# A spectral mixing layer and its MLP: 47 x 64 against 94 x 32 as the factors of the transform

## The chip, the core and the metric

One core of a Trainium2 chip runs the program. The metric is the device time of one execution in microseconds; for the kernel before it is the median of three runs.

## The reference

```python
def _attn_ref(x, filt_r, filt_i):            # x (8, 3008, 256)
    X = np.fft.rfft(x, axis=1)
    F = (filt_r + 1j * filt_i)[None, :, :]   # (1505, 256)
    return np.fft.irfft(X * F, n=x.shape[1], axis=1)

def _moe_ref(x, w_in, w_out, alpha):         # x (24064, 256), w_in (256, 2048), w_out (2048, 256)
    h = x @ w_in
    g = np.maximum(h, 0.0) + alpha * np.minimum(h, 0.0)
    return g @ w_out
```

Each of eight batches is filtered along its 3008 positions in the frequency domain, channel by channel. The 24064 rows that result go through a two-layer MLP whose activation has one negative slope per hidden unit.

## The kernel before

**The transform.** 3008 = 47 x 64. Stage A (piece_a, L158) multiplies by a 47-point table for two halves of the 64 positions at once (94 rows, 96 columns out). The result is saved to DRAM (save_a, L167) and read back turned (turn_a, L171), so that positions lie on partitions. Stage B (piece_b, L180) is a 64-point transform with the twiddles in its table, a 128-by-128 complex table per frequency k1, two k1 per piece, twelve pieces a batch. DVE multiplies the result in PSUM by the filter twice (L188, L189), once for the plain and once for the crossed parts; POOL's DMA swaps the two 64-partition halves of the crossed product (L191); piece_s (L194) adds it. Stage C (piece_c, L199) is the inverse 64-point transform; turn_c (L212) turns it through DRAM. Stage D (piece_d, L226) is the inverse 47-point transform and leaves the batch transposed in yT. ACT takes A, C and D out of PSUM.

**Batch 0** (class First, L246) is done alone at the start, without DRAM: its turns are matmuls with an identity (turn_at, piece_t), its B computes plain and crossed parts with tables of 64 columns (L281), its C multiplies by two tables (L298, L299). warm() issues matmuls with no use but to keep PE running.

**The MLP.** Tokens go in 48 blocks of 512 (384 in one of twelve). A block has 16 steps. At step j, Block.up (L409) makes hidden tile j: two matmuls of 512 columns (L414) into one half of a PSUM tile hps. After every odd j ACT copies both halves to SBUF as fp16 (L420, 128 x 1024), and DVE applies the slope (L423 twice, L424). Block.down (L427) of the block before runs in the same steps: each step does 4 of the 64 matmuls of 256 columns (L433) that make the output, 16 to a group of 128 tokens, two groups in one PSUM tile `op`. When a tile is full (j = 7 and j = 15 in a block of 512) ACT copies it to osb (L438) and SP's DMAs store it.

**Order.** The code is in manual schedule: engines run in the order in which the program records. A plan (put, plan_fft, L444 to L486) lists pieces by step; in the loop at L490 the pieces of a step are recorded first, then up, then down. One batch's transform is spread over about 150 steps, ahead of its MLP, which begins at step 96 b.

**PSUM.** It has eight banks, used as pools: psH (two tiles of two banks, hps), psO (two tiles of one bank, `op`), psF (two tiles of one bank, all pieces of the transform through bank(), L142). A new tile of a pool takes the next buffer in turn and waits for the readers of what was there.

Of the kernel before, what the change touches and what calls it, by code (L numbers as in the profile page):

```python
# [14 lines left out]
N1 = 47  # L15
N2 = 64
NK1 = 24
D = 256
NB = 8
DFF = 2048  # L20
NH = 32
# [4 lines left out]
def _build_consts():  # L26

    s1 = np.arange(N1)
    s2 = np.arange(N2)
    k1 = np.arange(NK1)
    p = np.arange(64)
    k2 = np.where(p < 32, p, 95 - p)
    g = np.where(p < 32, 1.0, -1.0)

    a1 = 2 * np.pi * np.outer(s1, k1) / N1
    wf1 = np.zeros((2 * N1, 96))  # L40
    wi3 = np.zeros((96, 2 * N1))
    scale = np.where(k1 == 0, 1.0, 2.0) / NFFT
    for h in range(2):
        r = slice(h * N1, h * N1 + N1)
        wf1[r, h * 48 : h * 48 + NK1] = np.cos(a1)
        wf1[r, h * 48 + NK1 : h * 48 + 48] = -np.sin(a1)
        wi3[h * NK1 : h * NK1 + NK1, r] = (np.cos(a1) * scale).T
        wi3[48 + h * NK1 : 48 + h * NK1 + NK1, r] = (-np.sin(a1) * scale).T

    kk = k1[:, None] + 47 * k2[None, :]  # L50
    ang = 2 * np.pi * s2[:, None, None] * kk[None, :, :] / NFFT
    c, s = np.cos(ang), np.sin(ang)
    twf = np.empty((128, NK1, 128))
    twf[:64, :, :64], twf[64:, :, :64] = c, s
    twf[:64, :, 64:], twf[64:, :, 64:] = -s * g, c * g
    ec, es = c.transpose(2, 1, 0), s.transpose(2, 1, 0)
    gp = g[:, None, None]
    twi = np.empty((128, NK1, 128))
    twi[:64, :, :64], twi[:64, :, 64:] = ec, es
    twi[64:, :, :64], twi[64:, :, 64:] = -es * gp, ec * gp  # L60
    return wf1, wi3, twf, twi
# [3 lines left out]
def kernel(  # L65
# [11 lines left out]
    wf1_np, wi3_np, twf_np, twi_np = _build_consts()  # L77
    wf1_d = nc.inline_tensor(wf1_np.astype(np.float16), name="c_wf1")
    wi3_d = nc.inline_tensor(wi3_np.astype(np.float16), name="c_wi3")
    twf_d = nc.inline_tensor(twf_np.astype(np.float16), name="c_twf")  # L80
    twi_d = nc.inline_tensor(twi_np.astype(np.float16), name="c_twi")
    twx_np = np.concatenate([twi_np[64:], -twi_np[:64]])
    twx_d = nc.inline_tensor(twx_np.astype(np.float16), name="c_twx")
    id_d = nc.inline_tensor(np.eye(128, dtype=np.float16), name="c_id")
    wfx_np = wf1_np.reshape(2 * N1, 2, 2, NK1).transpose(0, 3, 2, 1).reshape(2 * N1, 96)
    wfx_d = nc.inline_tensor(np.ascontiguousarray(wfx_np).astype(np.float16), name="c_wfx")
# [4 lines left out]
    p_uw = ctx.enter_context(tc.tile_pool(name="p_uw", bufs=3))  # L91
# [3 lines left out]
    psO = ctx.enter_context(tc.tile_pool(name="psO", bufs=2, space=bass.MemoryType.PSUM))  # L95
    psF = ctx.enter_context(tc.tile_pool(name="psF", bufs=2, space=bass.MemoryType.PSUM))
    dram = ctx.enter_context(tc.tile_pool(name="dram", bufs=1, space=bass.MemoryType.DRAM))
    a_dram = dram.tile([NB, 96, NH, D], FP16, name="a_dram")
    v_dram = dram.tile([NB, 96, NH, D], FP16, name="v_dram")
# [3 lines left out]
    wf1_s = konst.tile([2 * N1, 96], FP16, name="wf1_s")  # L103
    wi3_s = konst.tile([96, 2 * N1], FP16, name="wi3_s")
    twf_s = konst.tile([128, NK1, 128], FP16, name="twf_s")
    twi_s = konst.tile([128, NK1, 128], FP16, name="twi_s")
    filt_s = konst.tile([128, NK1, D], FP16, name="filt_s")
    filts_s = konst.tile([128, NK1, D], FP16, name="filts_s")
# [6 lines left out]
    wfx_s = konst.tile([2 * N1, 96], FP16, name="wfx_s")  # L115
    id16 = konst.tile([128, 128], FP16, name="id16")
    gtb = konst.tile([128, 17, 2, 512], FP16, name="gtb")
    twx_s = gtb[:, 14:17].rearrange("p a b c -> p (a b c)").rearrange("p (k m) -> p k m", m=128)
    yT = konst.tile([128, 2, 2 * NFFT], FP16, name="yT")

    def xrow(b, h, c):
        return bass.AP(tensor=x.tensor, offset=x.offset + (b * NFFT + NH * h + 8 * c) * D,
                       ap=[[N2 * D, N1], [1, 8 * D]])

    def load_x(b, c):
        xs = p_x.tile([2 * N1, 8 * D], FP16, name="xs")
        for h in range(2):
            nc.gpsimd.dma_start(out=xs[h * N1 : h * N1 + N1], in_=xrow(b, h, c))  # L128
        return xs

    def load_filt(dst, pbase, src, ka, kb):
        n = kb - ka
        nc.gpsimd.dma_start(
            out=dst[pbase : pbase + 32, ka:kb],
            in_=bass.AP(tensor=src.tensor, offset=src.offset + ka * D,
                        ap=[[47 * D, 32], [D, n], [1, D]]))
        nc.gpsimd.dma_start(
            out=dst[pbase + 32 : pbase + 64, ka:kb],
            in_=bass.AP(tensor=src.tensor, offset=src.offset + (N1 - ka) * D,
                        ap=[[47 * D, 32], [-D, n], [1, D]]))  # L140

    def bank(wide=False):  # L142
        if wide:
            return psH.tile([128, 2, 512], FP32, name="hps")[:, 0]
        return psF.tile([128, 512], FP32, name="psF")


    class Fft:
        def __init__(self, b):
            self.b = b  # L150
            self.base = (b % 2) * NFFT
            self.px, self.uw = {}, {}

        def start_a(self):
            self.asb = p_fft.tile([96, NH, D], FP16, name="asb")
            self.at = p_fft.tile([128, NK1, D], FP16, name="at")

        def piece_a(self, i, evict, wide=False):  # L158
            if i == 0:
                self.start_a()  # L160
            xs = xc[(self.b, i // 4)]
            ps = bank(wide)
            o = (i % 4) * 512
            nc.tensor.matmul(ps[0:96], wf1_s, xs[:, o : o + 512], start=True, stop=True)  # L164
            evict(self.asb[:, 2 * i : 2 * i + 2].rearrange("p a d -> p (a d)"), ps[0:96])
# [5 lines left out]
        def turn_a(self, eng, ka=0, kb=NK1):  # L171
            for h in range(2):
                for c in range(2):
                    r = h * 48 + c * NK1
                    q = c * 64 + NH * h
                    eng.dma_start(
                        out=self.at[q : q + NH, ka:kb],
                        in_=a_dram[self.b, r + ka : r + kb].rearrange("k s d -> s k d"))

        def piece_b(self, kp):  # L180
            px = bank().rearrange("p (k d) -> p k d", k=2)
            for kh in range(2):
                k1 = 2 * kp + kh
                nc.tensor.matmul(px[:, kh], twf_s[:, k1], self.at[:, k1], start=True, stop=True)  # L184
            uu = p_uw.tile([128, 2, D], FP16, name="uu", bufs=4)
            ww = p_uw.tile([128, 2, D], FP16, name="ww")
            sw = p_uw.tile([128, 2, D], FP16, name="sw")
            nc.vector.tensor_mul(ww, px, filts_s[:, 2 * kp : 2 * kp + 2])  # L188
            nc.vector.tensor_mul(uu, px, filt_s[:, 2 * kp : 2 * kp + 2])  # L189
            for o in (0, 64):  # L190
                nc.gpsimd.dma_start(out=sw[o : o + 64], in_=ww[64 - o : 128 - o])  # L191
            self.uw[kp] = uu, sw

        def piece_s(self, kp):  # L194
            uu, sw = self.uw[kp]
            nc.vector.tensor_add(uu, uu, sw)  # L196
            self.uw[kp] = (uu,)

        def piece_c(self, kp, evict, pv=None):  # L199
            if kp == 0:  # L200
                self.v = p_fft.tile([128, NK1, D], FP16, name="v")
                self.zt = p_fft.tile([96, NH, D], FP16, name="zt")
            us = self.uw.pop(kp)
            if pv is None:
                pv = bank().rearrange("p (k d) -> p k d", k=2)
            for kh in range(2):
                k1 = 2 * kp + kh
                for u in us:
                    nc.tensor.matmul(pv[:, kh], twi_s[:, k1], u[:, kh], start=u is us[0], stop=u is us[-1])  # L209
            evict(self.v[:, 2 * kp : 2 * kp + 2], pv)  # L210

        def turn_c(self, q):  # L212
            k = 6 * q
            for h in range(2):
                for c in range(2):
                    r = c * 48 + h * NK1 + k
                    p = c * 64 + NH * h
                    nc.sync.dma_start(
                        out=v_dram[self.b, r : r + 6].rearrange("k s d -> s k d"),
                        in_=self.v[p : p + NH, k : k + 6])  # L220
            if q == 3:
# [4 lines left out]
        def piece_d(self, i, evict, wide=False):  # L226
            g, dh, mh = i // 4, (i // 2) % 2, i % 2
            pd = bank(wide)
            ps = pd[:, 0 : 8 * N1].rearrange("p (m x) -> p m x", m=4)
# [3 lines left out]
            t0 = self.base + g * 752  # L233
# [117 lines left out]
    for i in range(16):  # L351
        f0.piece_a(i, both[i % 2], i % 2 == 1)
        if i % 4 == 3:
            warm((16, 6, 5, 8)[i // 4])
# [178 lines left out]
```

## Time and profile before

| | |
|---|---|
| median of three runs | 798.21 us (797.52 to 799.13) |
| the profiled execution, its span | 797.5 us |
| busy: PE, DVE, ACT, POOL | 98%, 81%, 75%, 18% |
| ACT: L420, 384 times | 385.4 us, 1004 ns each |
| DVE: L188 and L189, 84 times each | 57.4 and 57.1 us, 683 and 679 ns each |
| PE: L164 (A), L184 (B), L209 (C), L231 (D) | 42.6, 32.0, 33.4 and 41.9 us |
| start of the first L414 matmul | 39.37 us |
| granted PE clock, each slice | 9 (90% or more) |

Times of single instructions are those of the profile's groups; a PE matmul's row contains the drain after its last column, so matmuls that follow each other overlap in the rows. The profile numbers lines of the kernel. "PEld" is the load of a matmul's stationary operand. "Idle before" of a row is the time in which its engine stood still ahead of it, with what ended it.

### The profile page before, as it was taken

How to read it: one execution, taken by the hardware profiler on the slowest of the kernel's cores; microseconds unless marked ns; L12 is line 12 of the kernel's file. 1: busy time of each engine (PE TensorE's matmuls, PEld its weight loads, DVE VectorE, ACT ScalarE, POOL GpSimd, SP SyncE). 2: the span in 40 equal slices, each digit the busy share in tenths (PEclk: the TensorE clock that was granted, in tenths of full speed). 3: DMA queues.
4: the chain of work that ended last, by engine and by line, in shares of the span. 5: the costliest groups of instructions: out<-in, count | busy, mean ns of one | idle time of the engine just before them, and what ended most of it. 6: DMA issues, size and time to landing. Idle time of an engine off the chain costs nothing.

```text
span 797.5 us, 16176 instructions
## 1 busy us (share of the span) xinstructions
PE 778.6 (98%) x5980; PEld 542.8 (68%) x5980; DVE 645.7 (81%) x1449; ACT 597.6 (75%) x836; POOL 141.5 (18%) x272
## 2 busy tenths in 40 slices
PE   6999999999999999999999999999999999999997
PEld 6756667666667666766667666766666766776665
DVE  4787996798879987798877988799877999777773
ACT  3678678877778887788768877788877867686663
POOL 7511330132103210132102321032100221000000
PEclk9999999999999999999999999999999999999999
DMA  9967448574655447474483545754484243511111
GB/s 179 211 143 181 132 106 223 157 169 115 150 153 121 110 125 173 126 142 129 119 207 83 119 127 141 177 112 113 123 179 117 54 106 85 138 38 28 41 40 53
DMA packets 94360, 100.59 MB, mean 126 GB/s; under 512 B 11369, under 2 KB 82041, under 8 KB 94217
## 3 DMA queue, kind: packets, MB, share of 16 engines
q1 hardware_dynamic: 79512, 68.80, 32.8%
q0 software_dynamic: 14768, 30.75, 19.7%
q8 instruction: 47, 0.77, 0.4%
q14 instruction: 33, 0.26, 0.1%
HBM read 56.26 MB, written 46.66 MB: 129 GB/s over the span
## 4 chain that ended last, share of the span: by engine, by line
PE 90%; ACT 3%; DMA 2%; DVE 1%; issue 1%; SPq 1%; POOL 0%; ACTq 0%; DVEq 0%; POOLq 0%
PE op L433 39%; PE hps L414 39%; PE psF L164 3%; PE psF L231 3%; PE psF L209 2%; PE psF L184 2%; ACT gtb L420 2%; DMA xs<-in_x_dram 1%; DMA filt_s<-in_filt_i_dram 1%; ACT osb L438 1%; PE hps L281 1%; DMA a_dram<-asb 1%; ACT v L238 1%; SPq L396 1%; PE psF L310 1%
## 5 line engine op out<-in xcount | busy, mean ns | idle before, releaser
L420 ACT ACTIVATE gtb<-hps 128x1024 f16<-128x1024 f32 (+1 forms) x384 | 385.4, 1004 | 126.5 <-PE hps L414 126.1
L433 PE MATMUL op<-wout_s,gtb 128*128 128x256 f16 x3008 | 451.1, 272 | 0.6 <-DVE gtb L424 0.6
L414 PE MATMUL hps<-yT,win_s 128*128 128x512 f16 (+1 forms) x1536 | 449.1, 374 | 0.4 <-ACT gtb L420 0.2
L433 PEld LDWEIGHTS <-gtb 128*128 128x128 f16 x3008 | 293.2, 97 | 189.6 <-DVE gtb L424 0.9
L423 DVE TENSOR_SCALAR m<-gtb,alm_s 128x512 f16<-128x512 f16 (+1 forms) x768 | 237.9, 351 | 99.5 <-ACT gtb L420 97.3
L424 DVE TENSOR_TENSOR gtb<-gtb,m 128x1024 f16<-128x1024 f16 (+1 forms) x384 | 261.5, 681 | 24.8 <-PE hps L414 0.9
L191 POOL DMA_DIRECT2D sw<-ww x168 | 87.8, 527 | 483.8 <-DVE ww L188 480.9
L414 PEld LDWEIGHTS <-win_s 128*128 128x128 f16 x1536 | 144.9, 98 | 32.3 <-issue 4.3
L238 ACT ACTIVATE asb<-psF 96x512 f16<-96x512 f32 x112 | 66.5, 594 | 16.4 <-PE psF L164 16.3
L238 ACT ACTIVATE yT<-psF 128x376 f16<-128x376 f32 x120 | 58.1, 484 | 22.9 <-PE psF L231 22.5
L438 ACT ACTIVATE osb<-op 128x512 f32<-128x512 f32 x96 | 56.2, 585 | 6.1 <-issue 3.2
L188 DVE TENSOR_TENSOR ww<-psF,filts_s 128x512 f16<-128x512 f32 x84 | 57.4, 683 | 0.0
L189 DVE TENSOR_TENSOR uu<-psF,filt_s 128x512 f16<-128x512 f32 x84 | 57.1, 679 | 0.0
L238 ACT ACTIVATE v<-psF 128x512 f16<-128x512 f32 x84 | 50.0, 595 | 4.3 <-PE psF L209 4.3
L164 PE MATMUL psF<-xs,wf_s 94*96 94x512 f16 x112 | 42.6, 381 | 2.5 <-ACT v L238 2.1
L231 PE MATMUL psF<-wi_s,zt 96*128 96x94 f16 x504 | 41.9, 204 | 0.9 <-ACT yT L238 0.7
L128 POOL DMA_DIRECT2D xs<-in_x_dram x64 | 34.0, 542 | 29.6 <-PE psF L164 14.8
L231 PEld LDWEIGHTS <-zt 96*128 96x128 f16 x512 | 35.5, 97 | 5.1 <-issue 1.5
L184 PE MATMUL psF<-at,twf_s 128*128 128x256 f16 x168 | 32.0, 272 | 2.7 <-ACT v L238 1.7
L209 PE MATMUL psF<-uu,twi_s 128*128 128x256 f16 x168 | 33.4, 273 | 0.0
L196 DVE TENSOR_TENSOR uu<-uu,sw 128x512 f16<-128x512 f16 x72 | 30.1, 418 | 0.0
L209 PEld LDWEIGHTS <-twi_s 128*128 128x128 f16 x192 | 18.6, 98 | 2.8 <-DVE uu L189 0.4
(57 smaller groups left out, 200.0 us busy)
## 6 DMA issues: line engine op xcount, KB each, us to landing
out_dram<-osb SPq DMA_DIRECT2D x128, 128.0 KB
xs<-in_x_dram POOLq DMA_DIRECT2D x64, 188.0 KB, 4.4
a_dram<-asb SPq DMA_DIRECT2D x28, 384.0 KB
sw<-ww POOLq DMA_DIRECT2D x168, 64.0 KB, 2.1
v_dram<-v SPq DMA_DIRECT2D x112, 96.0 KB
zt<-v_dram SPq DMA_DIRECT2D x28, 384.0 KB
at<-a_dram SPq DMA_DIRECT2D x20, 384.0 KB
at<-a_dram SPq DMA_DIRECT2D x32, 96.0 KB
```

The source lines that it names most:

```text
L164: nc.tensor.matmul(ps[0:96], wf1_s, xs[:, o : o + 512], start=True, stop=True)
L188: nc.vector.tensor_mul(ww, px, filts_s[:, 2 * kp : 2 * kp + 2])
L191: nc.gpsimd.dma_start(out=sw[o : o + 64], in_=ww[64 - o : 128 - o])
L209: nc.tensor.matmul(pv[:, kh], twi_s[:, k1], u[:, kh], start=u is us[0], stop=u is us[-1])
L231: nc.tensor.matmul(ps[:, m], self.zt[:, 8 * g + 4 * mh + m, dh * 128 : dh * 128 + 128], wi3_s, start=True, stop=True)
L238: nc.scalar.activation(o, i, AF.Copy)
L414: nc.tensor.matmul(self.hps[:, j % 2, 0:tn], win_s[:, kt, j * 128 : (j + 1) * 128], yT[:, kt, self.t0 : self.t0 + tn], start=(kt == 0), st ...
L420: nc.scalar.activation(g[:, :, 0:tn], self.hps[:, :, 0:tn], AF.Copy)
L423: nc.vector.tensor_scalar(m[:, i, 0:tn], g[:, i, 0:tn], 0.0, a, OP.min, OP.mult)
L424: nc.vector.tensor_add(g[:, :, 0:tn], g[:, :, 0:tn], m[:, :, 0:tn])
L433: nc.tensor.matmul(self.op[:, si % 2], self.gts[k][:, 128 * si : 128 * si + 128], wout_s[:, k], start=(k == 0), stop=(k == 15))
L438: nc.scalar.activation(osb[:, 0:m], self.op[:, 0:m], AF.Copy)
```

## The change

- The factors are 94 and 32. Stage A has 94 inputs and gives real and imaginary parts for 24 frequencies of each parity; D is its inverse. Stages B and C are complex 32-point transforms, thus 64 by 64, two frequencies of each parity packed on 128 partitions, in array tiles of 64 rows and 64 columns: eight matmuls to a piece that covers four frequencies, six pieces a batch instead of twelve. Batch 0 uses tiles of 64 x 32 (B) and 64 x 128 (C).
- psF and psO are pools of one buffer. `psf` and `pso` are two-bank tiles made once; bank() and down() pick a half by a counter. turn_at, piece_b and pair_d (which replaces piece_d after batch 0) fill both banks of psf.
- piece_a (two matmuls, 1024 columns) and piece_c take a tile of psH, the ring of `up`, and are evicted as two banks by one ACT instruction; pair_d too, from psf.
- piece_b's two products and piece_s's sum are 1024 wide; the swap is four DMAs of 32 partitions. Batch 1 now adds with piece_s, where it accumulated C over both products.
- Six DMAs of tables are issued from ACT's queue during batch 0's stage A; the filter comes in chunks of eight DMAs of 16 partitions.
- The plan's steps are new.

```diff
-    psO = ctx.enter_context(tc.tile_pool(name="psO", bufs=2, space=bass.MemoryType.PSUM))
-    psF = ctx.enter_context(tc.tile_pool(name="psF", bufs=2, space=bass.MemoryType.PSUM))
+    psO = ctx.enter_context(tc.tile_pool(name="psO", bufs=1, space=bass.MemoryType.PSUM))
+    psF = ctx.enter_context(tc.tile_pool(name="psF", bufs=1, space=bass.MemoryType.PSUM))
...
+    psf = psF.tile([128, 2, 512], FP32, name="psF")
+    pso = psO.tile([128, 2, 2, D], FP32, name="psO")
...
     def bank(wide=False):
         if wide:
             return psH.tile([128, 2, 512], FP32, name="hps")[:, 0]
-        return psF.tile([128, 512], FP32, name="psF")
+        turn[0] += 1
+        return psf[:, turn[0] % 2]
...
+        def piece_a(self, i):
...
+            ps = psH.tile([128, 2, 512], FP32, name="hps")
+            for u in range(2):
+                o = (i % 2) * 1024 + 512 * u
+                nc.tensor.matmul(ps[0:96, u], wf1_s, xs[:, o : o + 512], start=True, stop=True)
+            on_act(self.asb[:, 4 * i : 4 * i + 4].rearrange("p a d -> p (a d)"),
+                   ps[0:96].rearrange("p a d -> p (a d)"))
...
+        def piece_b(self, q):
+            for h in range(2):
+                for par in range(2):
+                    r = slice(64 * par, 64 * par + 64)
+                    for e in range(2):
+                        k = 4 * q + 2 * h + e
+                        nc.tensor.matmul(psf[64 * e : 64 * e + 64, par, 256 * h : 256 * h + 256],
+                                         twf_s[r, k], self.at[r, k], start=True, stop=True)
...
+            nc.vector.tensor_mul(ww, px, fs)
+            nc.vector.tensor_mul(uu, px, f)
+            for o in range(0, 128, 32):
+                i = o ^ 32
+                nc.gpsimd.dma_start(out=sw[o : o + 32], in_=ww[i : i + 32])
...
+        def piece_c(self, q):
...
+            ps = psH.tile([128, 2, 512], FP32, name="hps")
+            for h in range(2):
+                for e in range(2):
+                    r = slice(64 * e, 64 * e + 64)
+                    for par in range(2):
+                        nc.tensor.matmul(ps[64 * par : 64 * par + 64, e, 256 * h : 256 * h + 256],
+                                         twi_s[r, 4 * q + 2 * h + par], u[r, par, h], start=True, stop=True)
+            on_act(self.v[:, 4 * q : 4 * q + 4].rearrange("p (h e) d -> p e h d", e=2),
+                   ps.rearrange("p e (h d) -> p e h d", h=2))
...
+        def pair_d(self, i):
+            g, dh = i // 2, i % 2
+            for mh in range(2):
+                self.inverse(psf[:, mh], g, dh, mh)
...
                 if si % 2 == 0 and k == 0:
-                    self.op = psO.tile([128, 2, D], FP32, name="op")
+                    self.op = pso[:, oturn[0] % 2]
+                    oturn[0] += 1
...
+    def d_steps(p):
+        return [p + t for t in (88, 91, 104, 108, 116, 120, 140, 152)]
...
+    for b in range(3, NB):
+        p = 96 * (b - 1)
+        a_at = [p - 96 + t for t in (6, 10, 18, 22, 30, 34, 42, 46)]
+        if b == 3:
+            a_at = [t + 6 for t in a_at]
+        plan_fft(b, a_at, p - 32, 1, [a_at[2 * c + 1] + 2 for c in range(4)],
+                 range(p + 2, p + 86, 12), 8, d_steps(p))
```

## The prediction, made before the changed kernel ran

> **What bounds the kernel now.** I read the page first (shares of the engines, chain, groups), then the timeline around an output eviction in the part without transforms, then two places in the head where a case of the new kernel already occurs. The page:
>
> ```profile
> span 797.5 us, 16176 instructions
> ...
> PE 778.6 (98%) x5980; PEld 542.8 (68%) x5980; DVE 645.7 (81%) x1449; ACT 597.6 (75%) x836; POOL 141.5 (18%) x272
> ...
> L433 PE MATMUL op<-wout_s,gtb 128*128 128x256 f16 x3008 | 451.1, 272 | 0.6 <-DVE gtb L424 0.6
> L414 PE MATMUL hps<-yT,win_s 128*128 128x512 f16 (+1 forms) x1536 | 449.1, 374 | 0.4 <-ACT gtb L420 0.2
> ```
>
> PE is busy 98% and its two big groups wait 1.0 us in all, and never on the output eviction L438. So PE's stream is the time: what makes PE stream less is gained in full, and each wait put into it is lost in full. I count L414 matmuls two to a step (768 steps). A 16-step block without transforms takes 13.89 us (742.90 to 756.79), 0.868 a step: up 0.435, down 0.435. Two batches (steps 192 to 384) run from 236.37 to 423.85, 187.48 us; 11.75 blocks of MLP are 163.2, so one batch's transform costs 12.1 us, nearly all of it matmul columns.
>
> **Cost 1: the output tile (psO).** The edit makes `pso` one two-bank tile whose halves are picked by a counter, where a pool of two tiles stood. In the built instruction stream of the changed kernel, 94 output groups begin with a `down` matmul that waits for ACT, and the count waited for is that of the `osb` eviction just before it, which reads the *other* half. The old stream has one such wait, and the profile shows no idle time from it. What this costs can be read here, in the part without transforms:
>
> ```profile
> 748.98 0.59 PE L414 MATMUL hps<-yT,win_s 128*128 128x512 f16 x2
> 749.41 0.60 PE L433 MATMUL op<-wout_s,gtb 128*128 128x256 f16 x4
> 749.61 1.02 ACT L420 ACTIVATE gtb<-hps 128x1024 f16<-128x1024 f32 x1 [0.71 <-PE hps L414]
> ...
> 749.85 0.59 PE L414 MATMUL hps<-yT,win_s 128*128 128x512 f16 x2
> 750.28 0.60 PE L433 MATMUL op<-wout_s,gtb 128*128 128x256 f16 x4
> 750.53 0.59 ACT L438 ACTIVATE osb<-op 128x512 f32<-128x512 f32 x1
> ```
>
> Let 0 be the end of the odd `up` (749.41). ACT starts the big eviction at 0.20 and holds it 1.02; `osb` stands behind it, from 1.12 to 1.71. PE has done `down` and the next `up` at 0.87 and now begins the next output group at once. With the wait it begins when osb is done, 0.05 later (the second view below): 1.76. The loss is 1.76 - 0.87 = 0.89 us, every eighth step. Behind the waiting matmul stands all of PE. With the shorter evictions of the 384-token blocks (0.81) the same sum gives 0.79 to 0.84. So 94 waits cost about 83 us, less what other work fits into them: a piece issued at a step 0 or 8 of a block runs before that `up` and is free up to 0.89.
>
> **Cost 2: pieces in the hps ring.** `piece_a` (now eight of two matmuls, 1024 columns) and `piece_c` take a buffer of psH, which has two and which `up` alternates. A piece at an even step takes the buffer that would be next, so the following `up` needs the buffer that ACT is still reading: in the stream, 94 `up`s wait for the eviction of the pair just before them, none in the old one. The head shows such a wait, where `up` runs without `down`:
>
> ```profile
> 46.93 1.94 ACT L420 ACTIVATE gtb<-hps 128x1024 f16<-128x1024 f32 x2 [0.85 <-PE hps L414]
> ...
> 48.00 1.94 PE L414 MATMUL hps<-yT,win_s 128*128 128x512 f16 x8 [0.25 <-ACT gtb L420]
> ```
>
> The first eviction ends at 46.93 + 1.02 = 47.95, PE goes on at 48.00: 0.05. So `up` cannot start before 0.20 + 1.02 + 0.05 = 1.27. PE has `down` (0.44) and piece_a (two of 512, 0.43) to fill that: it idles 0.40. A piece_a pair costs 1.27 - 0.44 = 0.84 instead of 0.43.
>
> **Gain: B and C in 64-by-64 tiles.** Columns fall from 12 x 2 x 256 to half, if four tiles run at once. The row nearest is the head's piece_b, two tiles of 128x64:
>
> ```profile
> 23.12 0.38 PE L271 MATMUL psF<-id,gtb 128*128 128x128 f16 x4
> 23.44 0.36 PEld L281 LDWEIGHTS <-twf_s 128*64 128x64 f16 x8
> 23.44 0.63 PE L281 MATMUL hps<-at,twf_s 128*64 128x256 f16 x8
> ...
> 23.99 0.10 PEld L298 LDWEIGHTS <-uu 128*128 128x128 f16 x1 [0.20 <-issue]
> ```
>
> Eight matmuls of 256 columns one by one would stream 0.87; they take 0.63 with a drain of 0.16 in it (four L433 last 0.60 where the next row starts 0.44 later), so 0.46: two at once. The last L271 (of four, 0.055 apart) streams to 23.34, so entering the tiled shape costs 0.10, leaving it another 0.10 (23.90 to 24.00). For four at once the bounds are 0.11 us a round of four (full) and 0.22 (only two at once); I take 0.11, since the pairs of this row hide each other fully. A group of B and C is then 4 rounds + 0.02 + 0.20 = 0.65 instead of 0.87. But C sits in the hps ring: 0.44 + 0.65 = 1.09 < 1.27, so the group ends at 1.27 all the same and costs 0.84. Seven groups a batch (the first, without C, 0.43): 5.5 us, against 24 x 0.218 = 5.2 before. The gain in columns is eaten by the wait.
>
> The Trainium skill (TensorEngine Tiling (Array Packing), Key Properties) says that tiles run loads and matmuls in parallel and that a change of tiling mode drains the engine. By that both 0.11 and the 0.10 at each end hold; with two at once the sum is the third rival's.
>
> **Hidden or small.** pair_d evicts 752 columns in one ACT instruction instead of two of 376; ACT has 25% free, and fewer, longer evictions save it about 0.1 us each. DVE: the fp32 products grow from 0.68 to about 1.2 for 1024 (the casts of 376 and 512 take 0.54 and 0.68, so 0.53 more for 512 more), six pairs instead of twelve: no longer in sum, cover is DVE's 19%. It fails only in batch 1, where products are added four steps later and six steps hold 3 x 1.31 + 2.3 + 0.7 = 7.0 us of DVE, with the swap's 4 x 0.52 issue and 2.1 landing: about 7.5 us per six steps against PE's 7.3. SP issues fewer output stores (no row or block is cut at 376 any more), POOL as many swap DMAs for the same bytes. The table loads move from POOL to ACT's queue, six issues among the early evictions, some 0.3 to 0.5 each (SP's issues at the start take 0.28 to 0.48), in a stretch where ACT idles.
>
> **The sum, by stage** (start of steps from L414):
> - Head, 39.4 before. The products take 12 x 1.15 instead of 24 x 0.6, but filters now need eight POOL issues a chunk (0.55 each) instead of four, and `psf` and `pso` as single tiles chain the evictions of turn, T and D: bounds 38 to 45, I take 42.
> - Steps 0 to 96, 101.7 before. Steps 16 to 32 hold eight piece_a: two steps become 1.27 + 0.43 + 0.44 + 0.35 (T) + 0.43 = 2.92, 23.4 against 20.9; the rest as above, with nine output waits and nine more piece_a or B and C groups at 0.84, and DVE's 7.5 per six steps from 48 to 80: 110.5.
> - Steps 96 to 192, 95.3 before: 81.6 MLP + 10.7 waits + 3.4 for four piece_a (four others fall into output waits) + 5.5 B and C + 2.8 = 104; the 2.8 is 1.3 for D and 1.5 at step 104, where piece_b wants `psf` while the eviction of a pair_d of the same step stands behind osb.
> - Each of the four batches in steps 192 to 576, 93.7 before: 81.6 + 12 x 0.89 + 8 x 0.84 + 5.5 + four pair_d outside the waits x 0.33 = 105.8, so 423 against 375.
> - Steps 576 to 672 (no piece_a): 87.3 becomes 99. To the end: 96.4 + twelve waits + 1.1 in the tail - 1.0 = 107.
>
> 42 + 110.5 + 104 + 423 + 99 + 107 = **885.5 us** of span; the median shown, 798.21, lies 0.7 above the span, so **886 us**.
>
> **Rivals.**
> 1. The output wait costs nothing, because the two halves lie in different banks. For: nothing else in the profile makes the halves meet. Against: the wait is in the stream, and the view at 48.00 shows PE stopping for just such a count. Time: 886 - 83 + 14 (pieces no longer hidden) = 817. The Trainium skill (PSUM — Partial Sum Buffer, PSUM bank collisions) asks to guard PSUM by bank and quadrant, and gives a bank 512 fp32: by it no wait is needed between the halves, so it speaks for this rival on what the chip allows, not on what was built.
> 2. Faster: ACT gets `osb` and the big eviction done before PE asks. Place: every eighth step and every psH piece; it decides if both end within 0.87 of the odd `up`, where the rows say 1.27 and 1.71. Then only columns count: six batches x (5.2 - 4.2) + 3.7 in batch 1 (which accumulated C twice), about 787.
> 3. The tiles do not run four at once: a group needs 1.5 instead of 1.27, +1.6 a batch, 897; with DVE's chain of batch 1 late too, 905.
>
> **How the numbers follow.** Forecast 0.80 (868 to 903), rival 3 0.10, rival 1 0.07, rival 2 0.03. The range takes the forecast's unknowns (head -4 to +3, waits 0.79 to 0.95 each, collisions +-6) and most of rival 3: 862 to 906. About 0.2% is what a measurement here can tell from no change; faster 0.03, same 0.01, slower 0.96.
>
> **What would show it.** In the profile after: idle time before the `down` matmul released by ACT osb, near 80 us in 94 waits; before `up`, released by ACT gtb, 25 to 35 us; PE's share under 90%; tiled matmuls starting in fours a few ns apart; DVE and ACT shares lower. Without idle at `down`, rival 1 is right; with fours 0.1 us apart in pairs, rival 3.

## The result, and the profile after

The changed kernel takes 898.34 us (median of four runs, 896.82 to 900.76) against 797.94 us for the kernel before: ratio 1.126, 95% interval 1.124 to 1.128. The profiled execution has a span of 895.0 us. The prediction said 886 us, 862 to 906.

First the page of the changed kernel, the lines that answer to the three of before (busy time and share of each engine; then group, busy us and mean ns, idle us ahead of the group and what ended it):

```profile
span 895.0 us, 16591 instructions
...
PE 792.5 (89%) x6484; PEld 519.9 (58%) x6484; DVE 642.5 (72%) x1325; ACT 588.8 (66%) x677; POOL 141.7 (16%) x284
...
L444 PE MATMUL psO<-wout_s,gtb 128*128 128x256 f16 x3008 | 451.8, 272 | 53.2 <-ACT osb L449 53.1
L424 PE MATMUL hps<-yT,win_s 128*128 128x512 f16 (+1 forms) x1536 | 451.3, 376 | 20.1 <-ACT gtb L430 15.7
```

The two big groups have nearly the same busy time as before (452 and 451 us against 451 and 449), so the matmuls themselves cost nothing new. What is new is on the right: 53.1 us of standing still before `down` (L444), ended by the eviction `osb`, and 15.7 us before `up` (L424), ended by the eviction `gtb`. Before, both columns together read 1.0 us. All shares fall, and ACT's share of 66% says nothing of the fact that PE now stands still for it 84 times ahead of `down` and 59 times ahead of `up`.

The view of PE's waits of the same kernel (what stood, what it waited for, us in total, times, longest) has these counts:

```profile
PE psO L444 <- ACT osb L449: 53.1, 84, 1.2
PE hps L424 <- ACT gtb L430: 15.7, 59, 0.6
PE hps L203 <- DVE uu L191: 4.9, 5, 1.6
```

One output wait, in the timeline of the changed kernel, in the part without transforms (start, us, what; in brackets the idle time ahead and its releaser):

```profile
848.94 0.60 PE L444 MATMUL psO<-wout_s,gtb 128*128 128x256 f16 x4
849.14 1.02 ACT L430 ACTIVATE gtb<-hps 128x1024 f16<-128x1024 f32 x1 [0.71 <-PE hps L424]
849.38 0.59 PE L424 MATMUL hps<-yT,win_s 128*128 128x512 f16 x2
850.07 0.59 ACT L449 ACTIVATE osb<-psO 128x512 f32<-128x512 f32 x1
...
850.71 0.60 PE L444 MATMUL psO<-wout_s,gtb 128*128 128x256 f16 x4 [0.73 <-ACT osb L449]
```

`up` starts at 849.38 and streams 0.43, so PE is ready at 849.82. The next `down` starts at 850.71, 0.05 after the end of `osb` (850.66). The loss is 0.89 us, the number of the prediction. The bracket says 0.73: a matmul's row is modelled to end 0.16 after its last column, and the idle column begins there. So 84 waits with 53.1 us listed are worth 53.1 + 84 x 0.16 = 66.5 us of the stream.

One wait of `up`, same kernel, a step with a piece_a:

```profile
270.37 0.60 PE L444 MATMUL psO<-wout_s,gtb 128*128 128x256 f16 x4
270.57 1.02 ACT L430 ACTIVATE gtb<-hps 128x1024 f16<-128x1024 f32 x1 [0.71 <-PE hps L424]
270.80 0.60 PE L152 MATMUL hps<-xs,wf_s 94*96 94x512 f16 x2
271.49 1.01 ACT L245 ACTIVATE asb<-hps 96x1024 f16<-96x1024 f32 x1
271.64 0.59 PE L424 MATMUL hps<-yT,win_s 128*128 128x512 f16 x2 [0.24 <-ACT gtb L430]
```

piece_a has streamed at 271.23 (270.80 + 0.43); `up` starts at 271.64, 0.05 after the eviction of the pair before it (271.59). PE loses 0.41; the prediction had 0.40.

Where the time sits by stage (us, from the starts of the `up` matmuls; "forecast" is the prediction's sum; e3 and e11 are told below):

| stage | before | forecast | after | e3 | e11 |
|---|---|---|---|---|---|
| head, to the first `up` | 39.4 | 42 | 42.8 | 44.7 | 40.8 |
| steps 0 to 96 | 101.7 | 110.5 | 114.9 | 112.4 | 98.9 |
| 96 to 192 | 95.3 | 104 | 106.6 | 97.3 | 95.7 |
| 192 to 576 (four batches) | 375.0 | 423 | 424.0 | 369.9 | 370.8 |
| 576 to 672 | 89.7 | 99 | 99.2 | 88.8 | 89.0 |
| 672 to the end | 96.4 | 107 | 107.6 | 96.5 | 96.4 |
| span | 797.5 | 885.5 | 895.0 | 809.6 | 791.6 |

Each measured column is one trace, and the early stages scatter between traces. e1 and e3 have the same code up to the first `up`, yet their heads take 42.1 and 44.7 us. Steps 0 to 16 scatter less: 16.0 to 16.3 us in the five kernels that have the same code there (the changed one, e1, e2, e3, e7).

### The profile page after: what moved, and what is told of

Same layout as the page of the kernel before. It is cut to its first block, busy times and chain, and to the rows that moved or that the text cites. A ratio compares the mean times of both kernels' runs of the same rounds, so it can differ in the third digit from the quotient of the medians.

```text
span 895.0 us, 16591 instructions
## 1 busy us (share of the span) xinstructions
PE 792.5 (89%) x6484; PEld 519.9 (58%) x6484; DVE 642.5 (72%) x1325; ACT 588.8 (66%) x677; POOL 141.7 (16%) x284
## 5 line engine op out<-in xcount | busy, mean ns | idle before, releaser
L444 PE MATMUL psO<-wout_s,gtb 128*128 128x256 f16 x3008 | 451.8, 272 | 53.2 <-ACT osb L449 53.1
L424 PE MATMUL hps<-yT,win_s 128*128 128x512 f16 (+1 forms) x1536 | 451.3, 376 | 20.1 <-ACT gtb L430 15.7
L444 PEld LDWEIGHTS <-gtb 128*128 128x128 f16 x3008 | 293.1, 97 | 252.4 <-issue 73.5
L424 PEld LDWEIGHTS <-win_s 128*128 128x128 f16 x1536 | 145.8, 98 | 69.4 <-issue 47.2
L449 ACT ACTIVATE osb<-psO 128x512 f32<-128x512 f32 x96 | 56.0, 583 | 7.7 <-issue 3.8
L245 ACT ACTIVATE asb<-hps 96x1024 f16<-96x1024 f32 x56 | 56.7, 1012 | 0.1
L245 ACT ACTIVATE yT<-psF 128x752 f16<-128x752 f32 (+1 forms) x64 | 48.5, 758 | 8.8 <-PE psF L225 8.8
L182 DVE TENSOR_TENSOR ww<-psF,filts_s 128x1024 f16<-128x1024 f32 x42 | 51.1, 1218 | 0.0
L183 DVE TENSOR_TENSOR uu<-psF,filt_s 128x1024 f16<-128x1024 f32 x42 | 51.0, 1215 | 0.0
L245 ACT ACTIVATE v<-hps 128x1024 f16<-128x1024 f32 x42 | 43.0, 1023 | 5.5 <-PE hps L203 5.5
L225 PE MATMUL psF<-wi_s,zt 96*128 96x94 f16 x504 | 33.2, 208 | 4.1 <-DVE uu L183 1.7
L225 PEld LDWEIGHTS <-zt 96*128 96x128 f16 x512 | 29.9, 100 | 8.0 <-issue 5.4
L152 PE MATMUL hps<-xs,wf_s 94*96 94x512 f16 x112 | 33.4, 379 | 0.2
L191 DVE TENSOR_TENSOR uu<-uu,sw 128x1024 f16<-128x1024 f16 x42 | 28.8, 686 | 2.7 <-DMA sw<-ww 2.6
L175 PE MATMUL psF<-at,twf_s 64*64 64x256 f16 x336 | 17.3, 281 | 1.1 <-ACT yT L245 1.1
```

Source lines behind the costliest of these rows:

```text
L182: nc.vector.tensor_mul(ww, px, fs)
L183: nc.vector.tensor_mul(uu, px, f)
L225: nc.tensor.matmul(ps[:, m], self.zt[:, 8 * g + 4 * mh + m, dh * 128 : dh * 128 + 128], wi3_s, start=True, stop=True)
L245: nc.scalar.activation(o, i, AF.Copy)
L424: nc.tensor.matmul(self.hps[:, j % 2, 0:tn], win_s[:, kt, j * 128 : (j + 1) * 128], yT[:, kt, self.t0 : self.t0 + tn], start=(kt == 0), st ...
L444: nc.tensor.matmul(self.op[:, si % 2], self.gts[k][:, 128 * si : 128 * si + 128], wout_s[:, k], start=(k == 0), stop=(k == 15))
```

## The experiments

The theory was the prediction's: two waits of PE for ACT (output tile, hps ring) make the loss, and the transform itself is a little cheaper than before. The rivals were that the waits only show where the time goes for another reason (then taking one away gives little), and that the tiled matmuls cost more than they save. Every kernel was timed against the kernel before, whose median was 797.8 to 798.0.

**e1_two_out.** The two halves of `pso` become two tiles of one bank, picked by the same counter.

```diff
-    pso = psO.tile([128, 2, 2, D], FP32, name="psO")
+    pso = [psO.tile([128, 2, D], FP32, name=f"psO{i}") for i in range(2)]
...
-                    self.op = pso[:, oturn[0] % 2]
+                    self.op = pso[oturn[0] % 2]
```

> The changed kernel with the two halves of pso as two tiles of one bank; all else as it is. Theory W (the output wait is the main loss): the idle time of the down matmul released by osb goes to almost nothing; a steady batch falls from 106.0 to 81.6 + 8 x 0.84 + 5.5 + 2.7 = 96.5 us, and the run to 820 to 832 us. Rival E (the wide evictions and the new plan of pieces hold ACT and so PE; the wait on osb only shows what ACT would cost anyway): PE then waits for ACT at up instead, and the run stays at 880 or more.

Measured: 832.82 us, ratio 1.045 (1.042 to 1.049); 65.5 us less than the changed kernel, and just above the 820 to 832 expected. Its list of PE's waits begins with the other wait; that of `down` for `osb` is gone:

```profile
PE hps L424 <- ACT gtb L430: 15.7, 59, 0.6
PE hps L203 <- DVE uu L191: 6.1, 5, 1.6
```

The stage without transforms falls from 107.6 to 96.5 us, the same as before the change; a batch of the middle falls from 106.0 to 96.7. Banks, counter, instructions and evictions are the same in both kernels. Only what counts as one tile differs, so the wait belongs to the tile and not to the chip.

**e4_before_one_out.** The same edit put alone into the kernel before, the other way round.

```diff
-    psO = ctx.enter_context(tc.tile_pool(name="psO", bufs=2, space=bass.MemoryType.PSUM))
+    psO = ctx.enter_context(tc.tile_pool(name="psO", bufs=1, space=bass.MemoryType.PSUM))
...
+    pso = psO.tile([128, 2, 2, D], FP32, name="psO")
...
+        return pso[:, oturn[0] % 2]
...
-                    self.op = psO.tile([128, 2, D], FP32, name="op")
+                    self.op = op_half()
```

> The kernel before with one edit of the change alone: the output tile is one tile of two banks whose half a counter picks. Theory W: 94 waits of 0.79 to 0.89 less pieces that fall into steps 0 and 8 of a block (about 1.5 us a batch): 865 to 880 us. Rival E: with the kernel before's short evictions the wait is met early, 798 to 815 us.

Measured: 869.30 us, ratio 1.089 (1.088 to 1.091), 71.5 us more than before. The list of its PE waits is led by

```profile
PE psO L440 <- ACT osb L445: 60.6, 95, 1.2
```

The whole change costs 100 us. This one line by itself, in the kernel before, costs 71.5; nothing of the new transform is needed for it.

**e2_down_first.** In steps with a piece in the hps ring, `down` is recorded before `up`, so PE has 0.43 us of other work while ACT reads the buffer that `up` needs.

```diff
+            ring.add(a_at[i])
...
+            if prev is not None and step in ring:
+                prev.down(j)
             blk.up(j)
-            if prev is not None:
+            if prev is not None and step not in ring:
                 prev.down(j)
```

> The changed kernel with down recorded ahead of up in the steps that hold a piece in the hps ring, so that PE has 0.44 us more work while ACT empties the buffer that up needs; the output tile stays one. Theory R (the ring wait costs 0.40 for a piece_a and 0.19 for a group of B and C): a steady batch falls by 8 x 0.40 + 6 x 0.19 = 4.3 us, the run by 20 to 27 us, to 872 to 879. Rival E: the eviction is only met later by the next up, and the run stays within 3 us of 898.

Measured: 878.66 us, ratio 1.101 (1.099 to 1.103), 19.7 us less than the changed kernel; a batch of the middle 101.9 instead of 106.0. PE's waits of `up` for `gtb` fall from 15.7 us to 0.4, and the list begins:

```profile
PE psO L444 <- ACT osb L449: 58.2, 90, 1.5
PE hps L203 <- DVE uu L191: 7.5, 6, 1.9
```

**e3_both.** e1 and e2 together.

> Both edits. If the two waits are separate and add up (W and R): 826 less 25 to 30, so 796 to 803 us, a steady batch near 92 us against 93.7 of the kernel before. If they hide each other (one ACT queue behind both): no lower than 815.

Measured: 811.06 us, ratio 1.016 (1.015 to 1.018), above the 796 to 803 expected if both costs add up and below the 815 of the other case. From e1 to e3 the order of `down` is worth 21.8 us, about what it was worth alone. Now a batch of the middle takes 92.5 us against 93.8 before: without the two waits the new transform is 1.3 us a batch cheaper. All that is lost against the kernel before now lies ahead of step 192, above all in the head (+5.3), the steps 0 to 16 (+5.5) and 48 to 80 (+6.7). So the two waits do add up, and the miss lies in those stages. The next experiments look there.

**e5_psf2.** e3 with `psf` as two tiles; piece_b's products are four of 512 instead of two of 1024, pair_d and turn_at evict bank by bank.

```diff
-    psf = psF.tile([128, 2, 512], FP32, name="psF")
+    psf = [psF.tile([128, 512], FP32, name=f"psF{i}") for i in range(2)]
...
-            nc.vector.tensor_mul(ww, px, fs)
-            nc.vector.tensor_mul(uu, px, f)
+            for r in range(2):
+                nc.vector.tensor_mul(ww[:, r], px[r], fs[:, r])
+            for r in range(2):
+                nc.vector.tensor_mul(uu[:, r], px[r], f[:, r])
```

> The kernel of both edits (two output tiles, down first in ring steps) with psf as two tiles of one bank too; the products and evictions that took two banks become two instructions of one bank. Theory P (in batch 0 the single psf tile makes each turn, T and D wait for the eviction of the other half): head and steps 0 to 16, 44.7 + 16.3, fall to 40 to 42 + 11 to 12.5, the run to 800 to 804 us; a steady batch stays within 0.5 of 92.2. Rival K (the halved clock of the first 55 us comes from waits for DVE and the filter's DMAs, not from psf): head and steps 0 to 16 stay within 1.5 us.

Measured: 806.95 us, ratio 1.010 (1.009 to 1.012), above the 800 to 804 expected. The head falls from 44.7 to 40.7 and steps 0 to 16 from 16.3 to 12.4: the same false wait as at the output, where a piece of batch 0 waits for the eviction of the piece before it, which lies in the other bank. The changed kernel shows it in steps 0 to 16 (timeline, PE's rows with a wait for an eviction in `psf`):

```profile
46.75 0.48 PE L324 MATMUL psF<-id,v 128*96 128x128 f16 x4 [0.72 <-ACT zt L245]
...
50.07 0.33 PE L225 MATMUL psF<-wi_s,zt 96*128 96x94 f16 x4 [0.70 <-ACT yT L245]
...
51.87 0.47 PE L225 MATMUL psF<-wi_s,zt 96*128 96x94 f16 x4 [1.04 <-DVE yT L248]
```

Of the 7.9 us gained there, 2.9 are given back in steps 48 to 80 (43.7 to 46.7), where DVE has four products to a piece instead of two; that this is the cause was not tested apart. One wait of 1.4 us stays in steps 0 to 16: a D piece there waits for DVE's eviction of its own bank.

**e6_hot.** e3 with 72 more matmuls without use in batch 0: 24 ahead of the loop, 8 in each of the five turns that have a B, 8 behind it (the expectations of e10 count them as 56; it is 72 there too).

```diff
     f0.turn_at(2, (on_act,))
+    warm(24)
...
             f0.piece_b(kp + 2)
+            warm(8)
             f0.piece_b(kp + 3)
...
-    warm(8)
+    warm(16)
```

> The kernel of both edits with more matmuls that only keep PE busy in batch 0: eight between two stage B pieces, 24 after the second turn, 16 instead of eight ahead of T. Theory K (the clock): the granted clock of the first 43 us rises from 0.78 to over 0.9 and that of steps 0 to 16 to 1.0; steps 0 to 16 fall from 16.3 to 13 or 14 us, the run to 805 to 808. Theory P: the clock rises, but the steps 0 to 16 stay over 15 us, since evictions, not columns, set them.

Measured: 809.18 us, ratio 1.014 (1.012 to 1.015), above the 805 to 808 expected. The stretches 0 to 43 and 43 to 59 us (columns: stretch, length, busy us and count of PE, PEld, DVE, ACT, POOL, then granted PE clock, DMA share, GB/s), first of the changed kernel:

```profile
0.00:43.00 43.00, 30.62 (x617) 25.00 (x618) 22.02 (x27) 19.27 (x31) 28.46 (x59) 0.78 0.99 170
43.00:59.00 16.00, 12.57 (x63) 5.99 (x62) 10.88 (x25) 10.02 (x13) 0.49 (x1) 0.83 0.44 100
```

then of e6_hot:

```profile
0.00:43.00 43.00, 32.75 (x684) 27.00 (x685) 21.54 (x26) 18.79 (x30) 27.91 (x58) 0.88 0.98 166
43.00:59.00 16.00, 12.20 (x81) 6.64 (x78) 11.62 (x27) 11.06 (x14) 0.98 (x3) 1.00 0.51 112
```

The kernel before has 0.96 in its head; e3, from which e6 departs, has 0.55 over 14 to 25 us and 0.50 over 34 to 45, as low as the changed kernel. With most of the clock back, the head and the steps 0 to 16 together take 58.3 us instead of the 61.0 of e3, 2.8 less. The 7.9 us of e5 cannot be set against this as they stand, for e5 has the clock back too, without added matmuls (0.88 over 0 to 43 us and 1.00 over 43 to 59, the same as e6). In steps 0 to 16, which scatter little, the clock alone takes 1.9 (16.3 to 14.4 in e6) and the split of `psf` at the same clock another 2.0 (to 12.4 in e5). The rest of e5's lead over e6, 3.2 us, lies in the head, which scatters by 2.6 from trace to trace. So which of the two is the larger part there is not shown; e5 shows that taking the chain away brings the clock back with it.

**e7_acc1.** e3 with batch 1 as before the change: C accumulates over both products (16 matmuls a piece, 8 steps behind B), piece_s is left out there, and the first two pair_d come at steps 92 and 94.

```diff
+                for u in us:
...
+                                             start=u is us[0], stop=u is us[-1])
...
-    plan_fft(1, range(16, 32, 2), 32, 4, (20, 24, 46, 50), range(42, 84, 6), 4, d_steps(0))
+    plan_fft(1, range(16, 32, 2), 32, 4, (20, 24, 46, 50), range(42, 84, 6), 0, [92, 94] + d_steps(0)[2:])
```

> The kernel of both edits with batch 1 as the kernel before has it: no piece_s, stage C accumulates over both products, eight steps behind stage B, and stage D's first two pieces four steps later. Theory D (batch 1 is held by DVE's products and sums and by the swap behind them): steps 48 to 80 fall from 43.7 to 38 to 40 us, the idle time of the stage C matmul released by the sum goes, the run to 805 to 808. Rival: PE's columns and the two stage A pieces set these steps, and four more rounds in each stage C make them 1 us longer.

Measured: 808.25 us, ratio 1.012 (1.010 to 1.014), at the upper end of the 805 to 808 expected. Steps 48 to 80 fall from 43.7 to 35.9 us, under the 37.1 of before. In e3 PE had stood there for DVE's sums:

```profile
PE hps L203 <- DVE uu L191: 9.4, 7, 2.2
```

In e7 that is gone, and this takes its place, in the steps 80 to 96, which grow from 13.0 to 19.3 us:

```profile
PE psF L227 <- DMA zt<-v_dram: 3.8, 1, 3.8
```

The last C is two steps later than with piece_s, and its way through DRAM ends after pair_d wants it. Of 7.9 us gained, 2.8 reach the end.

**e8_all.** e3 with the edits of e5, e6 and e7.

> All of it: two output tiles, down first, two psf tiles, more matmuls in batch 0, batch 1 accumulated in stage C. If P, K and D each hold for a part and add up: 788 to 796 us, under the kernel before, with 92.2 us for a steady batch. If the head stays as it is: 803 or more.

Measured: 805.00 us, ratio 1.009 (1.007 to 1.010), where 788 to 796 was expected if all parts add up. The gains do not add (4.1 + 1.9 + 2.8 would give 802.3): e6 and e5 heal the same stage, and the wait for `zt` is still there (4.0 us), with a clock of 0.81 around it:

```profile
128.00:146.00 18.00, 14.03 (x100) 10.05 (x99) 8.44 (x22) 9.54 (x14) 1.04 (x2) 0.81 0.73 182
```

**e9_early.** e8 with batch 1's B at closer steps, and batch 2's A moved out of C's way.

```diff
-    plan_fft(1, range(16, 32, 2), 32, 4, (20, 24, 46, 50), range(42, 84, 6), 0, [92, 94] + d_steps(0)[2:])
-    plan_fft(2, (44, 48, 54, 60, 66, 72, 78, 84), 86, 4, (70, 82, 94, 98),
+    plan_fft(1, range(16, 32, 2), 32, 4, (20, 24, 46, 50), (42, 46, 52, 56, 62, 66, 72), 0, [92, 94] + d_steps(0)[2:])
+    plan_fft(2, (44, 48, 58, 68, 72, 76, 80, 84), 86, 4, (70, 82, 94, 98),
```

> The kernel of e8_all with batch 1's B pieces begun at steps 42, 46, 52, 56, 62, 66 (C 8 steps behind, so at 50 to 74 where e8_all has 50 to 80), and batch 2's A pieces moved out of C's way. Theory T (what is left of the loss of e8_all in the steps 80 to 192 is the way of batch 1's last C through DRAM: pair_d waits 4.0 us for zt, and the granted clock falls with PE standing still): the wait for zt goes or falls under 1 us, the steps 80 to 192 fall from 119.1 us to 112 to 114, the time from 805.0 to 798 to 801. Theory U (the clock and the steps 96 to 192 suffer from the denser pieces of batches 1 and 2, not from the wait): the steps 80 to 192 stay above 117, 803 to 805; and if DVE becomes late at the spacing of 4 and 6 steps, the steps 48 to 80 grow from 35.9 by 2 or more.

Measured: 798.19 us, ratio 1.000 (0.999 to 1.001): as fast as the kernel before. The wait for `zt` is gone, the steps 80 to 192 fall from 119.1 to 111.2, and the same stretch of the trace has its clock back (the two edits of the plan were not tried apart):

```profile
128.00:146.00 18.00, 17.89 (x144) 12.99 (x142) 11.94 (x33) 13.76 (x20) 1.03 (x2) 1.00 0.73 198
```

**e10_early_cool.** e9 without the added matmuls of e6.

> e9_early without the 56 added warm matmuls of batch 0. If those matmuls cost more time in PE's stream of the head than the clock gives back (head 40.71 us in e5_psf2 without them, 42.06 in e8_all with them), 1 to 1.5 us less than e9_early: 797 to 799.5, which is the kernel before within 0.2%. If they pay, the same or up to 1 more than e9_early.

Measured: 798.58 us, ratio 1.001 (0.999 to 1.002): no difference from e9 that can be told, and a head of 42.5 instead of 41.7 us. The expectation that the added matmuls cost a microsecond failed. Why the head took 40.7 us in e5 and 42.1 in e8 stays open; each kernel's head is known from one trace only, and these 1.4 us are less than the 2.6 between e1 and e3.

**e11_spread.** e9 with batch 0's second quarter of D two steps apart and two of batch 1's pair_d two steps later, away from the piece_b at step 114.

```diff
-    for g, t0, d0, gap, evs in ((1, 0, 6, 1, both), ...
+    for g, t0, d0, gap, evs in ((1, 0, 6, 2, both), ...
...
-    plan_fft(1, ..., (42, 46, 52, 56, 62, 66, 72), 0, [92, 94] + d_steps(0)[2:])
+    plan_fft(1, ..., (42, 46, 52, 56, 62, 66, 72), 0, [92, 94, 104, 108, 118, 122, 140, 152])
```

> The kernel of e9_early with two waits of PE taken out by later steps: batch 0's four D pieces of the second quarter at steps 6, 8, 10, 12 where they were at 6, 7, 8, 9 (one of them stands 1.44 us for a psF bank that DVE evicts late), and batch 1's pair_d at steps 118 and 122 where they were at 116 and 120 (the one at 116 stands 1.7 us for DVE's products of the piece_b at 114). If both waits cost what they show: 1.4 + 1.7 = 3.1 us less than e9_early, so a span near 792.7 and about 795, which is 0.3 to 0.4% faster than the kernel before. If what stands late is DVE and not the bank, the waits move on to the next pieces and the time stays at 797 to 798.5, within 0.2% of the kernel before.

Measured: 794.48 us, ratio 0.996 (0.995 to 0.997): 0.4% under the kernel before, which is little, but more than the interval. The page:

```profile
span 791.6 us, 17003 instructions
...
PE 770.6 (97%) x6604; PEld 518.6 (66%) x6604; DVE 638.2 (81%) x1403; ACT 587.6 (74%) x738; POOL 143.4 (18%) x284
```

PE's busy time is 8 us under the 778.6 of before. Of the two waits, the one for DVE's products went (steps 96 to 192: 98.1 to 95.7). The one for DVE's `yT` did not: its row still shows 1.5 us, and steps 0 to 16 gained only 0.4. The rest of the 4.2 us by which the span fell lies in the head (0.9) and in steps 48 to 64 (0.7), which this edit does not explain; e9 and e10, whose code is the same in steps 48 to 64, differ there by 1.2.

## Why the prediction was right, and what it mis-sized

- **Cost 1, the output tile: right.** 0.89 us a wait was forecast and is in the trace. Net of the pieces that hide in it, the prediction had 83 - 14 = 69 us (rival 1's 817 against 886); e1 measures 65.5. Alone in the kernel before it is 71.5.
- **Cost 2, the hps ring: right.** 0.41 against 0.40 for a piece_a; e2 and e3 give 19.7 and 21.8 us for all of it. In a batch of the middle it is 4.2 (e1 to e3), where the terms of the prediction give 8 x 0.40 for the A pieces and 5.5 - 4.2 for B and C, 4.5 in all.
- **Gain, the 64-by-64 tiles: right.** The prediction gave 5.2 - 4.2 = 1.0 us a batch without the waits; e3 measures 1.3 for the whole batch, with the new A and D pieces in it. In the trace the first four matmuls of a B start at 280.742, .745, .748 and .752, the next four at 280.875, C's at 280.984 and 281.093: four at once, and a round of 256 columns takes 0.109 once it flows (0.133 for the first). So rival 3 is out.

```profile
280.21 0.60 PE L444 MATMUL psO<-wout_s,gtb 128*128 128x256 f16 x4
280.74 0.41 PE L175 MATMUL psF<-at,twf_s 64*64 64x256 f16 x8
280.98 0.39 PE L203 MATMUL hps<-uu,twi_s 64*64 64x256 f16 x8
281.49 0.59 PE L424 MATMUL hps<-yT,win_s 128*128 128x512 f16 x2
```

  The last 128-by-128 matmul starts at 280.539 and streams 0.109, so entering the tiled shape costs 0.094; after C's last round (281.202) the next weight load starts at 281.301, 0.099 later. The forecast had 0.10 for each. The Trainium skill (TensorEngine Tiling (Array Packing), Key Properties) says that a change of tiling mode drains the array; the trace agrees, with these two numbers.
- **Rival 1** is out for the kernel as built: `down` waits in 84 rows. What it said of the chip holds: in e1 PE writes one of the two banks (775.28 to 775.72) while ACT reads the other (775.54 to 776.13), and no wait is there, as the Trainium skill (PSUM — Partial Sum Buffer, PSUM bank collisions) has it with its guard by bank and quadrant. The wait comes from following a two-bank tile as one thing.
- **Rival 2** is out: ACT ends `osb` where the rows said, at 1.72 after the odd `up` (848.94 to 850.66), not within 0.87. Its price was also added wrongly: 6 x 1.0 + 3.7 under 798.2 is 788.5, not 787.
- **The sum, 9.5 us short in the span.** 4.4 of it are in steps 0 to 96. The step that failed is "the rest as above": the prediction let single tiles chain the evictions in the head alone and names no term for steps 0 to 16, 10.8 us before. They take 16.2, because the same `psf` still carries eight pieces of batch 0 there (e5: 3.9 us less with two tiles), of which e6 puts 1.9 down to the halved clock. The other steps of this stage miss both ways: 2.7 us more than forecast in 48 to 80 (below), 0.9 less in 16 to 32, and about 2.8 less in the rest. Another 2.6 us are in steps 96 to 192. A wait that the prediction left out lies there: a D matmul (L225) stands 1.7 us until DVE's products (L183) have left `psf`. In e9 such waits come to 1.7 us again, and in e11, which moves the piece two steps later, they are gone and the stage is 2.4 us shorter. The other stages are within 1 us each. The prediction's 87.3 us for steps 576 to 672 of the kernel before was misread; it is 89.7. Its forecast of 99 does not hang on it, for the other terms give it (81.6 + 10.7 + 5.5 + 1.3).
- **From span to median** the prediction added 0.7 us, as before. It is 3.3 here: the profiled execution, 896.82, was the fastest of four that spread over 3.9 us. That is 2.6 of the 12.3 us between 886 and 898.3.
- **The signs:** PE's share is 89%, and tiled matmuls start in fours. The idle times came out under the signs named: 53.1 us in 84 waits before `down` (near 80 in 94 was named) and 15.7 in 59 before `up` (25 to 35); with 0.16 added to each they are 66.5 and 25.1.
- **Hidden or small:** DVE's chain in batch 1 was named as 7.5 us per six steps against PE's 7.3. The path was right and the size too small: steps 48 to 80 take 42.7 us, thus 8.0 per six steps and 5.6 in all more than before, and e7 (from e3's 43.7) shows that with accumulation instead they take 35.9. The table loads on ACT's queue were not tested alone.

## What to carry to other kernels

Where two halves of a buffer are to alternate, make them two tiles: one tile with a counter had the same banks and the same instructions, and cost 65.5 us in the changed kernel and 71.5 in the old one, in 84 and 95 waits, most of them of 0.8 to 0.9 us, on the engine that sets the time. A piece that borrows a buffer from a two-deep ring needs work of its own length behind it on PE; here exchanging two calls in fourteen steps a batch was worth 4.2 us a batch. And price a wait at the pace of the stream: a wait taken away in one stage (batch 1's sums, 7.9 us) came back as another (`zt`, 3.8 us and a slower clock) until the next deadline was moved too.

## What was not expected of the hardware

The granted clock. In the changed kernel it is 0.53 on average over 14 to 25 us and again over 34 to 45 us, while PE's rows still show 8.8 and 8.4 of 11 us as busy:

```profile
14.00:25.00 11.00, 8.78 (x161) 6.52 (x161) 6.65 (x9) 4.11 (x7) 9.79 (x20) 0.53 0.96 168
34.00:45.00 11.00, 8.35 (x88) 6.83 (x88) 3.85 (x6) 4.49 (x9) 2.70 (x6) 0.53 1.26 207
```

The half clock holds from 14.2 to 24.5, 34.7 to 44.9 and 51.8 to 55.2 us: 10.2, 10.2 and 3.4 us. So busy rows alone do not show it: a matmul at half clock has a longer row (an `up` pair 1.06 us at 42.78, 0.59 later). The Trainium skill (TensorE: Matmul & The Clock Gate, Part 1: The HAM clock gate) speaks of a free-running window of about 3.4 us after which an idle array is halved; the lengths here are 3, 3 and 1 times that. But PE was not idle ahead of them: in the 3.41 us before each of the three its rows cover 2.04, 1.40 and 1.69 us. The same holds in all thirteen traces, read without 10 us at each end, in stretches of 3.41 us in step with the clock's changes: the half clock begins only behind stretches in which PE's rows cover 31 to 64%, and no stretch under 49% went without it. In e8 it came far behind the head as well, at the one wait of 4.0 us (it ends at 140.97, and the half clock begins at 139.2; 0.81 over 18 us), and in e9, without that wait, the same stretch is at 1.00.
